# Two chunks instead of one at each visit of a linear-attention and MLP kernel to its attention part

## The chip, the cores and the metric

The kernel runs on one core of a Trainium2 chip. The metric is the device time of one execution in microseconds (us). Before the change its median over three runs is 209.67 us (209.66 to 209.96).

The engines are named as in the profile: PE (matmuls; PEld is its weight load), ACT (activations and copies), DVE and POOL (elementwise work; POOL also issues the loads from memory), and SP (issues transposing DMAs and the stores).

## The reference

```python
# attention, per batch b and head h, blocks of 64 positions, state kept from block to block
intra = (qb @ kb.T * Dmask) @ vb           # Dmask: lam ** (i - j) for i >= j, else 0
inter = (qb * lam_pow) @ kv_state
out[:, :, sl] = intra + inter
kv_state = lam_block * kv_state + (kb * rev_pow).T @ vb
...
x = out.transpose(0, 2, 1, 3).reshape(B * S, H * D)      # 3072 tokens x 512
g = gelu(x @ w_in)                                       # exact gelu, 512 -> 2048
return g @ w_out                                         # 2048 -> 512
```

q, k and v are 4 batches x 8 heads x 768 positions x 64; the output is 3072 x 512 in float32. The kernel works in bf16 with float32 sums.

## The kernel before, in words

**Chunks and groups.** The kernel cuts a sequence into chunks of 128 positions. A chunk is one of 4 batches at one of 6 places in the sequence, with all 8 heads, so there are 24 chunks, numbered 4 * place + batch. Four chunks make a group: 512 tokens. The MLP of group g runs on PE while the attention of group g + 1 is slipped in between its blocks of matmuls. Chunks 0 and 1 come before group 0's first block, chunks 2 and 3 between its first blocks.

**MLP blocks.** `mlp_blocks` gives a list of blocks. For groups 1 to 5 these are 16 blocks of the first matrix product (`mm1`: four matmuls of 512 columns into a PSUM bank of the tag `mh`, which has two banks, then a GELU on ACT that empties it, lines 412 and 416) and 14 blocks of `blocks_by_seven` (the second product, done by seven products of half size; 8 matmuls of 256 columns each, line 306; their sums run on DVE). That is 30 blocks, and each counts 2048 in a running cost called `done`. Group 0 has 21 blocks of the first product, then 16 of the second (`mm2`, four matmuls of 512 columns, line 426).

**The attention of one chunk** (n) has these steps:

- `begin` and `dma_transposes` (185-189): SP issues two transposing DMAs, `kT` and then `qT`, from the loaded k and q. Both have three buffers. Chunks 0 to 7 are transposed on PE instead (`transposed`, line 169).
- `decay_v` (163): POOL makes `v_dec` (7 buffers).
- `scores` (191-200): 8 matmuls on half of the array's rows (line 196) into two banks of the tag `sc`; then `masked` twice, a DVE product each (204), which gives `sc_m`.
- `outputs` (222-235): 4 matmuls with the state over the whole array (226) and 8 matmuls on half of the array's columns with `v_dec` and `sc_m` (231), into a bank of the tag `o`; then `empty_outputs` writes the chunk's part of x, by ACT for chunks 0 to 7 (239) and by DVE for the others (241).
- `next_state` (206-220): 4 matmuls (211) into the bank of the tag `t`, and two DVE operations.
- `prefetch` (453): POOL issues the loads of k, q and v of the chunk four numbers on (67).

**What sets the order.** The program is written out by hand: each engine executes its instructions in the order in which Python emits them. For group 0 the dictionary `group0` (546) says before which block a step stands. For the rest, `todo` (568-575) is a sorted list of (place, step, chunk), and a step is emitted before the first block whose `done` has reached its place; `place(g + f)` is the point at the fraction f of group g's blocks. The scores of group g + 1's four chunks stand at four places spread over group g (fractions 0.06 to 0.795 for g > 1, 0.21 to 0.81 for g = 1). Outputs of a chunk stand where the scores of the next one stand, and the last outputs at 0.93. `begin` stands 0.32 of a group ahead of the chunk's scores. The outputs of chunk 7 open group 1, whose first block is split by columns so that its first part does not need chunk 7.

Of the kernel before, what the change touches and what calls it, by code (L numbers as in the profile page):

```python
# [8 lines left out]
F32 = mybir.dt.float32  # L9
BF16 = mybir.dt.bfloat16  # L10
# [5 lines left out]
def kernel(  # L16
# [10 lines left out]
    nc = tc.nc  # L27
# [137 lines left out]
    def transposed(c, name, tag, empty):  # L165

        src, t_ps = getattr(c, name), bank([128, HP, C], BF16, tag, "t_ps")
        for hp in range(HP):
            nc.tensor.transpose(t_ps[:, hp, :], src[:, 2 * hp:2 * hp + 2, :], ident)  # L169
# [14 lines left out]

    def dma_transposes(c):
        c.kT = work_pool.tile([128, HP, C], BF16, tag="kT", name="kT")
        c.qT = work_pool.tile([128, HP, C], BF16, tag="qT", name="qT")
        nc.sync.dma_start_transpose(out=c.kT, in_=c.k.rearrange("p h d -> p (h d)"))
        nc.sync.dma_start_transpose(out=c.qT, in_=c.q.rearrange("p h d -> p (h d)"))

    def scores(c):
        sc_ps = [bank([128, HP, C], F32, "sc", f"sc_ps{hi}") for hi in range(2)]
        for hp in range(HP):
            for hi in range(2):
                p = slice(hi * D, (hi + 1) * D)
                nc.tensor.matmul(sc_ps[hi][:, hp, :], c.kT[p, hp, :], c.qT[p, hp, :], start=True, stop=True)  # L196
        c.sc_m = work_pool.tile([128, HP, 2, C], BF16, tag="sc_m", name="sc_m")
        c.sc_ps = sc_ps
        for hi in range(0 if c.n == 0 else 2):
            masked(c, hi)  # L200

    def masked(c, hi):
# [16 lines left out]
            nc.vector.tensor_mul(new, tmp, lam_blk)  # L219
        states[c.n + M] = new  # L220

    def outputs(c, x_t, off, evacuate=True):
        o_ps = bank([128, HP, C], F32, "o", "o_ps")
        if c.sb > 0:
            for hp in range(HP):
                nc.tensor.matmul(o_ps[:, hp, :], states[c.n][:, hp, :], c.qT[:, hp, :],  # L226
                                 start=(hp == 0), stop=False, skip_group_check=True)
        v = c.v if c.early else c.v_dec
        for hi in range(2):
            for hp in range(HP):  # L230
                nc.tensor.matmul(o_ps[hi * D:(hi + 1) * D, hp, :], v[:, 2 * hp + hi, :], c.sc_m[:, hp, hi, :],  # L231
                                 start=(c.sb == 0 and hp == 0), stop=True, skip_group_check=True)
        c.x_o, c.o_ps = x_t[:, :, off * C:(off + 1) * C], o_ps
        if evacuate:
            empty_outputs(c)

    def empty_outputs(c):
        if c.n < 2 * M:
# [28 lines left out]
    def blocks_by_seven(g, g_t, first):  # L267
# [22 lines left out]
                    g_sum((5, 2, 1, 6, 7)[i - 10], 0)  # L290
            return both

        paired = [kf for k in range(KH) for kf in (k, k + KH)]
        blocks = [(with_sums(i, first[kf][0]), first[kf][1]) for i, kf in enumerate(paired)]
# [103 lines left out]
    def mlp_blocks(g):  # L398
        T = M * C
        x_t = xT[g]  # L400
        g_t = g_pool.tile([128, NK2, T], BF16, tag="g", name="g_t")

        def mm1(kf, ks=1, cols=slice(0, T)):
            n = cols.stop - cols.start

            def run():
                h_ps = bank([128, ks, n], F32, "mh", "h_ps")
                parts = [(0, T - C), (T - C, T)] if g == 1 and kf == 0 else [(0, n)]
                for k in range(ks):
                    for lo, hi in parts:  # L410
                        for ki in range(NK1):
                            nc.tensor.matmul(h_ps[:, k, lo:hi], w_in_t[:, ki, (kf + k) * 128:(kf + k + 1) * 128],  # L412
                                             x_t[:, ki, cols.start + lo:cols.start + hi],
                                             start=(k == 0 and lo == 0 and ki == 0), stop=(ki == NK1 - 1),
                                             skip_group_check=True)
# [73 lines left out]
    causal(1)  # L489
    keep_warm(2)  # L490
    scores(c)
    for hi in range(2):
        masked(c, hi)
# [5 lines left out]
    outputs(live[0], xT[0], 0)  # L499
# [5 lines left out]
    outputs(live[1], xT[0], 1)  # L505
    c = early(2)
    transposed(c, "k", "mh", copy)
    transposed(c, "q", "mo", copy)
# [31 lines left out]
    x1 = lambda n: outputs(live[n], xT[1], n - M)  # L540
# [4 lines left out]
    e = N1  # L545
    group0 = {
        1: [lambda: scores(live[2])],
        5: [lambda: outputs(live[2], xT[0], 2)],
        6: [lambda: next_state(live[0])],
        7: [lambda: next_state(live[1])],  # L550
        8: [lambda: both_transposed(live[3])],
        9: [lambda: next_state(live[2])],
        10: [lambda: scores(live[3])],
        12: [lambda: outputs(live[3], xT[0], 3)],
        17: [lambda: next_state(live[3])],
        e: [w_out_sums, lambda: decay_v(live[4], nc.vector)],
        e + 8: [lambda: transposes(live[4])],
        e + 9: [lambda: scores(live[4])],
        e + 10: [lambda: x1(4), lambda: transposes(live[5])],
        e + 11: [lambda: scores(live[5])],  # L560
        e + 12: [lambda: x1(5), lambda: transposes(live[6])],
        e + 13: [lambda: scores(live[6])],
        e + 14: [lambda: x1(6), lambda: transposes(live[7])],
        e + 15: [lambda: scores(live[7])],
    }

    BEGIN, STATE, SCORES, OUTPUTS = 0, 1, 2, 3
    todo = [(total, -OUTPUTS, 2 * M - 1)]
    for n in range(2 * M, NCH):
        g, i = n // M - 1, n % M  # L570
        first, apart = (0.21, 0.2) if g == 1 else (0.06, 0.245)
        at = first + apart * i
        todo += [(place(g + at - (0.28 if n == 2 * M else 0.32)), -BEGIN, n), (place(g + at), -SCORES, n),
                 (place(g + (at + apart if i < M - 1 else 0.93)), -OUTPUTS, n)]
    todo += [(place(n // M + (0.01, 0.12, 0.18, 0.24)[n % M]), -STATE, n) for n in range(M, NCH - M)]
    todo.sort()

    def step(minus_kind, n):
        kind = -minus_kind
        if kind == BEGIN:  # L580
            live[n] = begin(n)
            dma_transposes(live[n])
            decay_v(live[n], nc.gpsimd)
        elif kind == SCORES:
            scores(live[n])
            prefetch(n + M)
        elif kind == STATE:
            next_state(live[n])
        else:
            outputs(live[n], xT[n // M], n % M)  # L590

    done = 0
    for g in range(NG):
        if g + 1 < NG:
            alloc_x(g + 1)
        for i, (run, cost) in enumerate(mlp_blocks(g)):
# [1 line left out]
                for act in group0.get(i, []):  # L598
                    act()
            while todo and todo[0][0] <= done:  # L600
                step(*todo.pop(0)[1:])
            run()
            done += cost
        for item in [t for t in todo if t[2] // M == g + 1 and t[1] != -STATE]:
            todo.remove(item)
            step(*item[1:])


# [28 lines left out]
```

## Time and profile before

| | |
|---|---|
| median of three runs | 209.67 us (209.66 to 209.96) |
| the profiled execution's own time | 209.99 us |
| its span, first to last instruction | 208.2 us |
| PE busy | 200.3 us, 96% of the span |
| DVE / POOL / ACT busy | 139.0 / 97.1 / 81.7 us |
| group 1's first MLP block starts | 53.5 us |
| groups 2, 3, 4, 5 start | 84.9, 116.0, 147.1, 178.1 us |
| bytes moved by DMA | 24.65 MB in 102370 packets |

The span is 1.8 us shorter than the execution's own time; what lies around it belongs to launch and end. Busy matmuls overlap in the records (a matmul is 379 ns long but the next one starts 216 ns after it), so lengths on PE are taken from start to start, or from the chain of waits, which cuts the overlaps. A few matmul records are missing in the trace, so a piece shown as x7 may have held 8.

### The profile page before, as it was taken

The page shows a single profiled execution, that of the slowest core. Times are in us where ns is not written, and L with a number is a line of the kernel's source. Part 1 is how long each engine was busy: PE and PEld are TensorE (multiplying, and loading weights), DVE is VectorE, ACT ScalarE, POOL GpSimd, SP SyncE. Part 2 cuts the span into 40 slices and gives each one's busy share as a digit, 9 for nine tenths or more (in the row PEclk, how much of TensorE's full clock was granted, in tenths as well). Part 3 has the DMA queues.
Part 4 walks back from the last instruction along what each step waited for, and adds up shares of the span by engine and source line. Part 5 has one row for each costly group of instructions (what it writes and reads, how often), then busy time and mean ns, then how long its engine had stood idle before and what let it go on. Part 6 is the DMA issues. An engine that isn't in the chain of part 4 may idle for free.

```text
span 208.2 us, 4142 instructions
## 1 busy us (share of the span) xinstructions
PE 200.3 (96%) x1708; PEld 130.5 (63%) x1725; DVE 139.0 (67%) x220; ACT 81.7 (39%) x145; POOL 97.1 (47%) x112
## 2 busy tenths in 40 slices
PE   7889999999999999999999999999999999999992
PEld 2457574465555788654688554688555688544881
DVE  4744525855476789889779689579678579123482
ACT  4966563324555410265420265410365410466200
POOL 8999953799998995499300493000200000000000
PEclk9999999999999999999999999999999999999999
DMA  5999999999999999999930699100651000500014
GB/s 116 155 174 177 200 207 188 154 215 148 151 177 154 153 150 154 233 141 175 155 25 3 219 134 175 29 0 3 227 103 29 0 0 3 201 0 0 3 50 151
DMA packets 102370, 24.65 MB, mean 118 GB/s; under 512 B 92880, under 2 KB 99536, under 8 KB 102352
## 3 DMA queue, kind: packets, MB, share of 16 engines
q0 software_dynamic: 80688, 13.37, 90.2%
q1 hardware_dynamic: 21664, 11.02, 23.5%
q8 instruction: 13, 0.21, 0.4%
q14 instruction: 5, 0.04, 0.1%
HBM read 27.27 MB, written 6.29 MB: 161 GB/s over the span
## 4 chain that ended last, share of the span: by engine, by line
PE 86%; POOL 8%; DVE 3%; issue 1%; POOLq 0%; DVEq 0%
PE h_ps L412 39%; PE p_ps L306 9%; PE r_ps L306 8%; PE q_ps L306 8%; PE o_ps L426 7%; PE o_ps L231 4%; PE s_ps L306 3%; PE sc_ps L196 3%; PE kv_ps L211 3%; POOL w_in_t L88 3%; PE o_ps L226 2%; POOL k_t L67 2%; POOL q_t L67 2%; POOL v_t L67 2%; PE t_ps L169 1%
## 5 line engine op out<-in xcount | busy, mean ns | idle before, releaser
L416 ACT ACTIVATE g_t<-h_ps 128x512 bf16<-128x512 f32 (+2 forms) x101 | 58.2, 576 | 81.2 <-PE h_ps L412 81.0
L412 PE MATMUL h_ps<-x_t,w_in_t 128*128 128x512 bf16 (+3 forms) x446 | 88.7, 343 | 0.6
L412 PEld LDWEIGHTS <-w_in_t 128*128 128x128 bf16 x460 | 40.2, 98 | 36.0 <-issue 0.6
L163 POOL TENSOR_TENSOR v_dec<-v_t,lam_m 128x512 bf16<-128x512 bf16 x23 | 25.2, 1101 | 44.5 <-PE kv_ps L211 42.9
L306 PEld LDWEIGHTS <-g_sum 128*128 128x128 bf16 x400 | 38.6, 98 | 5.2
L281 DVE TENSOR_TENSOR g_sum<-g_t 128x1024 bf16<-128x1024 bf16 x50 | 33.6, 716 | 11.3 <-ACT g_t L416 11.3
L204 DVE TENSOR_TENSOR sc_m<-sc_ps,cmask 128x512 bf16<-128x512 f32 x40 | 25.6, 680 | 2.0 <-PE sc_ps L196 2.0
L67 POOL DMA_DIRECT2D v_t<-in_v_dram x24 | 21.4, 893 | 3.3 <-DMA w_out_t<-in_moe_w_out_dram 2.9
L67 POOL DMA_DIRECT2D k_t<-in_k_dram x24 | 22.2, 924 | 1.7 <-DMA w_out_t<-in_moe_w_out_dram 1.4
L67 POOL DMA_DIRECT2D q_t<-in_q_dram x24 | 21.6, 898 | 2.1 <-DMA w_out_t<-in_moe_w_out_dram 2.1
L306 PE MATMUL r_ps<-w_sum,g_sum 128*128 128x256 bf16 x160 | 19.3, 273 | 0.1
L241 DVE TENSOR_TENSOR x_t<-o_ps,lam_q 128x512 bf16<-128x512 f32 x16 | 11.0, 687 | 10.2 <-PE o_ps L231 10.2
L306 PEld LDWEIGHTS <-g_t 128*128 128x128 bf16 x160 | 15.3, 98 | 3.2
L218 DVE TENSOR_TENSOR tmp<-kv_ps,state 128x512 f32<-128x512 f32 x16 | 11.0, 689 | 7.8 <-PE kv_ps L211 7.8
L426 PE MATMUL o_ps<-w_out_t,g_t 128*128 128x512 bf16 x61 | 14.8, 380 | 0.1
L219 DVE TENSOR_TENSOR state<-tmp,lam_blk 128x512 bf16<-128x512 f32 x16 | 14.4, 901 | 0.5
L306 PE MATMUL p_ps<-w_sum,g_t 128*128 128x256 bf16 x80 | 10.1, 273 | 0.0
L196 PE MATMUL sc_ps<-qT,kT 64*128 64x128 bf16 x192 | 9.5, 218 | 0.3 <-DVE qT L172 0.3
L306 PE MATMUL q_ps<-w_sum,g_t 128*128 128x256 bf16 x80 | 9.7, 273 | 0.0
L470 PE MATMUL idle_ps<-idle 128*128 128x256 bf16 (+1 forms) x33 | 8.4, 393 | 1.2 <-DVE idle L101 1.2
L426 PEld LDWEIGHTS <-g_t 128*128 128x128 bf16 x64 | 5.8, 98 | 6.1
L306 PE MATMUL p_ps<-w_out_t,g_sum 128*128 128x256 bf16 x80 | 9.6, 273 | 0.0
(65 smaller groups left out, 168.0 us busy)
## 6 DMA issues: line engine op xcount, KB each, us to landing
out_dram<-o_sb SPq DMA_DIRECT2D x9, 512.0 KB, 2.8
k_t<-in_k_dram POOLq DMA_DIRECT2D x24, 128.0 KB, 5.9
q_t<-in_q_dram POOLq DMA_DIRECT2D x24, 128.0 KB, 6.1
v_t<-in_v_dram POOLq DMA_DIRECT2D x24, 128.0 KB, 6.2
w_out_t<-in_moe_w_out_dram POOLq DMA_DIRECT2D x4, 512.0 KB, 11.1
w_in_t<-in_moe_w_in_dram POOLq DMA_DIRECT2D x7, 256.0 KB, 7.5
out_dram<-o_sb SPq DMA_DIRECT2D x5, 256.0 KB, 5.7
wide_w<-in_moe_w_in_dram SPq DMA_DIRECT2D x1, 512.0 KB, 4.2
```

What stands on the lines that cost most here:

```text
L67: nc.gpsimd.dma_start(raw[n, name], chunk_of(name, n))
L163: eng.tensor_mul(c.v_dec, c.v, lam_m[:, :, None].to_broadcast((128, H, D)))
L196: nc.tensor.matmul(sc_ps[hi][:, hp, :], c.kT[p, hp, :], c.qT[p, hp, :], start=True, stop=True)
L204: nc.vector.tensor_mul(c.sc_m[:, :, hi, :], c.sc_ps[hi], mask)
L218: nc.vector.tensor_add(tmp, kv_ps, states[c.n])
L219: nc.vector.tensor_mul(new, tmp, lam_blk)
L241: nc.vector.tensor_mul(c.x_o, c.o_ps, lam_q)
L281: nc.vector.tensor_tensor(gsum[i][:, ks, :], g_t[:, ka + k:ka + k + n4, ta], g_t[:, kb + k:kb + k + n4, tb], op=op)
L306: nc.tensor.matmul(o, left[i](k, slice(u * C, (u + 1) * C)), right[i](k), start=(begin and k == 0), stop=(k == KH - 1), skip_group_check=True)
L412: nc.tensor.matmul(h_ps[:, k, lo:hi], w_in_t[:, ki, (kf + k) * 128:(kf + k + 1) * 128], x_t[:, ki, cols.start + lo:cols.start + hi], start ...
L416: nc.scalar.activation(g_t[:, kf:kf + ks, cols], h_ps, ACT.Gelu)
L426: nc.tensor.matmul(om[io], g_t[:, kf, io * C:(io + 1) * C], w_out_t[:, kf, :], start=(kf == 0), stop=(kf == NK2 - 1))
```

## The change

`visit(done, asked)` takes the place of single steps: it emits the outputs of the chunks in `done` (all the matmuls with states, then all those with values, then the emptying) and then the scores of the chunks in `asked`, and after these their four masks, last chunk first, and their prefetches. For this the second chunk's scores go to banks of other tags (`mo`, `mh`, or `t` and `o`) and the second chunk's outputs to `t`. `qT` gets a fourth buffer. B is one block of 30.

- Group 0: chunks 4 and 5 get their scores before block e + 10 and their outputs before e + 13; chunks 6 and 7 get their scores before e + 15.
- Group 1: the first six pairs of `mm1` blocks become 12 half blocks of 256 columns: six on the columns of chunks 4 and 5, then the outputs of chunks 6 and 7 (at 3B), then six on the columns of 6 and 7. Scores of 8 and 9 at 8B; outputs of 8, 9 and scores of 10, 11 at 20B; outputs of 10, 11 and scores of 12, 13 at 26B.
- Groups 2, 3 and 4: outputs of the first two chunks and scores of the last two at 9B; outputs of these and scores of the next group's first two at 26B (in group 4 the outputs alone).
- Of the scores made at 26B, the masks stand apart: at 26B, 28B, and at 1B and 2B of the next group.
- `begin` of a group's first two chunks stands at 0.57 and 0.60 (before the block at 18B) of the group before, that of its last two at 0.00 and 0.04 of the group itself; for chunks 8 to 11 at -0.07, 0, 0.13 and 8B.

```diff
-        dst = work_pool.tile([128, HP, C], BF16, tag=name + "T", name=name + "T")
+        dst = work_pool.tile([128, HP, C], BF16, tag=name + "T", name=name + "T", bufs=4 if name == "q" else 3)
...
-    def scores(c):
-        sc_ps = [bank([128, HP, C], F32, "sc", f"sc_ps{hi}") for hi in range(2)]
+    def scores(c, tags="sc sc", mask=True):
+        sc_ps = [bank([128, HP, C], F32, tag, f"sc_ps{hi}") for hi, tag in enumerate(tags.split())]
...
+    def outputs(*chunks):
+
+        for c, tag in zip(chunks, ("o", "t")):
+            from_states(c, tag)
+        for c in chunks:
+            from_values(c)
+        for c in chunks:
             empty_outputs(c)
...
-            return blocks_by_seven(g, g_t, [(mm1(kf), 4 * T) for kf in range(NK2)])
+            paired = [kf for k in range(NK2 // 2) for kf in (k, k + NK2 // 2)]
+            plan = [(kf, 1, slice(0, T)) for kf in paired]
+            if g == 1:
+                plan = [(kf, 1, slice(0, T // 2)) for kf in paired[:6]]
+                plan += [(kf, 1, slice(T // 2, T)) for kf in paired[:6]] + [(kf, 1, slice(0, T)) for kf in paired[6:]]
...
         e + 8: [lambda: transposes(live[4])],
-        e + 9: [lambda: scores(live[4])],
-        e + 10: [lambda: x1(4), lambda: transposes(live[5])],
-        e + 11: [lambda: scores(live[5])],
-        e + 12: [lambda: x1(5), lambda: transposes(live[6])],
-        e + 13: [lambda: scores(live[6])],
-        e + 14: [lambda: x1(6), lambda: transposes(live[7])],
-        e + 15: [lambda: scores(live[7])],
+        e + 9: [lambda: transposes(live[5])],
+        e + 10: [lambda: visit([], [4, 5], "t o")],
+        e + 11: [lambda: transposes(live[6])],
+        e + 13: [lambda: visit([4, 5], [])],
+        e + 14: [lambda: transposes(live[7])],
+        e + 15: [lambda: visit([], [6, 7], "t o")],
...
+    def visit(done, asked, banks="mo mo", mask=True):
+        outputs(*[live[n] for n in done])
+        for n, tags in zip(asked, ("sc sc", banks)):
+            scores(live[n], tags, mask=False)
+        for n in reversed(asked if mask else []):
+            for hi in range(2):
+                masked(live[n], hi)
+        for n in asked:
             prefetch(n + M)
...
+    B = 1 / (NK2 + 14)
+    for g in range(1, NG - 1):
+        n = (g + 1) * M
+        for i, w in enumerate((0.11, 0.14, 0.19, 0.24) if g == 1 else (0.01, 0.12, 0.18, 0.24)):
+            at(g + w, lambda i=i, g=g: next_state(live[g * M + i]))
+        if g == 1:
+            for i, w in enumerate((-0.07, 0.0, 0.13)):
+                begin_at(g + w, n + i)
+            visit_at(g + 8 * B, [], [n, n + 1])
+            begin_at(g + 8 * B, n + 3)
+            visit_at(g + 20 * B, [n, n + 1], [n + 2, n + 3], banks="mh mh")
         else:
+            for i in (2, 3):
+                begin_at(g + (i - 2) * 0.04, n + i)
+            visit_at(g + 9 * B, [n, n + 1], [n + 2, n + 3])
+        later_on = [n + M, n + M + 1] if g < NG - 2 else []
+        for i, c_n in enumerate(later_on):
+            begin_at(g + 0.57 + 0.03 * i, c_n)
+        visit_at(g + 26 * B, [n + 2, n + 3], later_on, masks=(g + 26 * B, g + 28 * B, g + 1 + 1 * B, g + 1 + 2 * B))
+    at(1 + 3 * B, lambda: visit([2 * M - 2, 2 * M - 1], []))
```

More of the change, by code (lines that the diff above doesn't have):

```diff
@@ L198, in scores @@
         c.sc_ps = sc_ps
-        for hi in range(0 if c.n == 0 else 2):
+        for hi in range(2 if mask else 0):
             masked(c, hi)
@@ L220, in next_state, with from_states, from_values @@
         states[c.n + M] = new
-    def outputs(c, x_t, off, evacuate=True):
-        o_ps = bank([128, HP, C], F32, "o", "o_ps")
+    def from_states(c, tag):
+        c.o_ps = bank([128, HP, C], F32, tag, "o_ps")
         if c.sb > 0:
             for hp in range(HP):
-                nc.tensor.matmul(o_ps[:, hp, :], states[c.n][:, hp, :], c.qT[:, hp, :],
+                nc.tensor.matmul(c.o_ps[:, hp, :], states[c.n][:, hp, :], c.qT[:, hp, :],
                                  start=(hp == 0), stop=False, skip_group_check=True)
+    def from_values(c):
         v = c.v if c.early else c.v_dec
@@ L291, in with_sums @@
             return both
-        paired = [kf for k in range(KH) for kf in (k, k + KH)]
-        blocks = [(with_sums(i, first[kf][0]), first[kf][1]) for i, kf in enumerate(paired)]
+        done = [cost for _, cost in first]
+        blocks = [(with_sums((sum(done[:i]) + 4 * M * C - 1) // (4 * M * C), run), cost)
+                  for i, (run, cost) in enumerate(first)]
         left = {1: lambda k, t: gsum[1][:, k, t], 2: lambda k, t: gsum[2][:, k, t],
@@ L407, in run @@
                 h_ps = bank([128, ks, n], F32, "mh", "h_ps")
-                parts = [(0, T - C), (T - C, T)] if g == 1 and kf == 0 else [(0, n)]
                 for k in range(ks):
[L410 to L415, printed above, removed]
+                    for ki in range(NK1):
+                        nc.tensor.matmul(h_ps[:, k, :], w_in_t[:, ki, (kf + k) * 128:(kf + k + 1) * 128],
+                                         x_t[:, ki, cols], start=(k == 0 and ki == 0), stop=(ki == NK1 - 1),
+                                         skip_group_check=True)
                 nc.scalar.activation(g_t[:, kf:kf + ks, cols], h_ps, ACT.Gelu)
@@ L498 @@
     transposed(c, "q", "mo", copy)
-    outputs(live[0], xT[0], 0)
+    outputs(live[0])
     nc.scalar.copy(w_in_t[:, :, :256], wide_w)
@@ L504 @@
     make_lam_blk()
-    outputs(live[1], xT[0], 1)
+    outputs(live[1])
     c = early(2)
@@ L557, with at, begin_at, run @@
         e + 8: [lambda: transposes(live[4])],
-        e + 9: [lambda: scores(live[4])],
-        e + 10: [lambda: x1(4), lambda: transposes(live[5])],
-        e + 11: [lambda: scores(live[5])],
-        e + 12: [lambda: x1(5), lambda: transposes(live[6])],
-        e + 13: [lambda: scores(live[6])],
-        e + 14: [lambda: x1(6), lambda: transposes(live[7])],
-        e + 15: [lambda: scores(live[7])],
-    }
[L567 to L580, printed above, removed]
+        e + 9: [lambda: transposes(live[5])],
[4 more added lines that the diff above has]
+        e + 15: [lambda: visit([], [6, 7], "t o")],
+    }
+    todo = []
+    def at(when, run):
+        todo.append((place(when), run))
+    def begin_at(when, n):
+        def run():
             live[n] = begin(n)
@@ L583, in step, with visit_at @@
             decay_v(live[n], nc.gpsimd)
-        elif kind == SCORES:
-            scores(live[n])
-            prefetch(n + M)
-        elif kind == STATE:
-            next_state(live[n])
-        else:
-            outputs(live[n], xT[n // M], n % M)
+        at(when, run)
+    def visit(done, asked, banks="mo mo", mask=True):
[6 more added lines that the diff above has]
+        for n in asked:
+            prefetch(n + M)
+    def visit_at(when, done, asked, banks="mo mo", masks=None):
+        at(when, lambda: visit(done, asked, banks, masks is None))
+        if masks:
+            for w, (n, hi) in zip(masks, [(n, hi) for n in asked for hi in range(2)]):
+                at(w, lambda n=n, hi=hi: masked(live[n], hi))
+    B = 1 / (NK2 + 14)
[9 more added lines that the diff above has]
+            visit_at(g + 20 * B, [n, n + 1], [n + 2, n + 3], banks="mh mh")
+        else:
+            for i in (2, 3):
[6 more added lines that the diff above has]
+    at(1 + 3 * B, lambda: visit([2 * M - 2, 2 * M - 1], []))
+    todo.sort(key=lambda t: t[0])
     done = 0
@@ L600 @@
             while todo and todo[0][0] <= done:
-                step(*todo.pop(0)[1:])
+                todo.pop(0)[1]()
             run()
             done += cost
-        for item in [t for t in todo if t[2] // M == g + 1 and t[1] != -STATE]:
-            todo.remove(item)
-            step(*item[1:])
+    assert not todo
 _INS = ['q', 'k', 'v', 'lam', 'moe_w_in', 'moe_w_out']
```

17 lines of the change are left out of this document (8 added, 9 removed).

## The prediction, made before the changed kernel was run

> **What bounds the kernel now.** I read the engines' busy shares first, then the chain of waits, then the waits of PE, then SP's queue.
>
> ```profile
> PE 200.3 (96%) x1708; PEld 130.5 (63%) x1725; DVE 139.0 (67%) x220; ACT 81.7 (39%) x145; POOL 97.1 (47%) x112
> ```
>
> PE is never long without work, and in all it waits for others for under 3 us by the records. So the time is the length of PE's stream, and the change counts by what it takes out of the stream and by the waits that it puts in. The granted clock is 0.998, so no durations change with it. The chain of waits (start, length, what) shows what an attention visit costs in group 2:
>
> ```profile
> 86.12 0.86 PE h_ps L412 x4
> 86.98 0.33 PE sc_ps L196 x8
> 87.31 1.83 PE h_ps L412 x8
> 89.14 0.22 PE kv_ps L211 x4
> 89.37 1.73 PE h_ps L412 x8
> ...
> 101.19 0.87 PE p_ps L306 x8
> 102.06 0.22 PE o_ps L226 x4
> 102.28 0.35 PE o_ps L231 x8
> 102.64 0.33 PE sc_ps L196 x8
> 102.97 0.98 PE p_ps L306 x8
> ```
>
> Four matmuls of 128 columns over the whole array take 0.22 (kv_ps). Eight on half of the rows (sc_ps) or columns (o_ps L231) take 0.33 and 0.35: less than 0.44, so two halves run side by side (0.22), and 0.11 to 0.13 is the price of changing the array's shape. Changing back costs 0.10 more (1.83 against 1.73, 0.98 against 0.87). So scores alone cost 0.33 + 0.10 = 0.43, outputs with scores 0.22 + 0.35 + 0.33 + 0.11 = 1.01, outputs alone 0.22 + 0.35 + 0.11 = 0.68.
>
> **What the change takes out.** From chunk 4 on, the kernel before has 8 scores alone, 8 outputs alone, 12 of both: 8 x 0.43 + 8 x 0.68 + 12 x 1.01 = 21.0 us. In group 0's tail the values also wait for their masks:
>
> ```profile
> 49.27 0.22 PE o_ps L226 x4
> 49.50 0.57 PE o_ps L231 x8
> 50.06 0.55 PE t_ps L169 x8
> ```
>
> Here L231 takes 0.57 instead of 0.35. This happens four times (0.55, 0.56, 0.57, 0.57), and once in group 1 (0.54 at 82.58): 1.0 us of stalls. Now there are 3 pairs of scores alone, 3 pairs of outputs alone and 7 visits with both. A second chunk adds 0.22 for each of its steps while the shape stays; with a change of shape of its own it would add up to 0.35 for each half-array step (2.4 us in all). I take 0.22, since the 0.10 to 0.13 show only where the shape changes. So 3 x 0.65 + 3 x 1.12 + 7 x 1.68 = 17.1 us. The gain is 21.0 + 1.0 - 17.1 = **4.9 us**, and the masks of group 0's pairs (four DVE products, one every 0.60, done 2.6 after the scores) now have 3.6 us, so nothing replaces these stalls.
>
> **What group 1's start adds.** Group 0's tail begins at 39.49 as before. It holds 8 blocks (6.91), 4 transposes (1.80), 2 pairs of scores (1.30), 1 pair of outputs (1.12): group 1 starts at 50.6.
> (a) Half blocks. In group 0 sixteen matmuls of 256 columns start at 15.50 and are over at 17.55, 2.05 us, where 16 x 0.109 = 1.75. Two banks: the fourth matmul starts 0.33 into a block, lasts 0.27, GELU takes 0.38, and hand-overs 0.09, so a bank returns after 1.07 while two half blocks take 0.87. The first six lose 0.2 twice, and some 0.05 behind the last copy of group 0; of the second six three next_state matmuls fill all but 0.2. Together 0.65; they run 50.6 to 53.7.
> (b) Outputs of 6 and 7 (to 54.8) stand right before blocks that read their x. ACT copies both, 0.59 each and 0.49 apart (50.10, 50.58), the first from 54.7; x is there at 55.8. PE waits 1.0; queued behind it are all later blocks.
> (c) Second half blocks, 2.62 + 0.67 (next_state) + 0.2, to 59.3; two whole blocks and a next_state, 1.95: the visit for 8 and 9 comes at 61.3, the scores of 9 at 61.6. They need chunk 9's qT:
>
> ```profile
> 53.87 1.37 SPq L188 DMA_TRANSPOSE kT<-k_t  x1
> 55.43 1.88 SPq L189 DMA_TRANSPOSE qT<-q_t  x1
> ```
>
> This is SP's timeline (start, time on SP). The DMA view gives the time from issue to landing, first for that qT, then for one issued at 153.05, when no loads run:
>
> ```profile
> qT<-q_t SPq DMA_TRANSPOSE x1, 9.0
> ...
> qT<-q_t SPq DMA_TRANSPOSE x1, 2.4
> ```
>
> So chunk 9's qT lands at 64.4. Before, nobody noticed: chunk 9's scores stood at 66.83. The issue is not set by PE: SP issues chunk 8's pair at 49.53 and 50.93 when its loads have landed, then group 0's last two stores, then these. POOL's loads up to chunk 11 are issued by 55.7 in either kernel. Moving POOL's v_dec of chunk 10 ahead of chunk 12's loads (58.2 before, some 60.9 after) comes too late to help. PE waits 64.4 - 61.6 = **2.8 us**, and behind it stand group 1's other 22 blocks. Bounds: 0, if qT lands in under 6.2; 3.5, if it takes as long again as the spread of 7.6 to 9.0 seen around it. Since (c) ends at a fixed moment, errors in (a) and (b) are swallowed by it.
>
> [...]
>
> **What the later visits add.** SP's order again: each transpose takes 1.2 to 1.4 there, and behind these wait only the stores at a group's end.
> (d) Chunks 12 and 13 are begun at 18B of group 1, but qT of 12 reuses chunk 8's buffer and kT of 13 that of chunk 10, both free only in the visit at 20B. With the visit's start as 0: SP issues at 0.4, 1.8, 3.1; the scores of 13 come at 1.68 + 6 x 0.873 + 1.34 = 8.3. Chunk 13's qT may take 5.1. Landings were 6.6 to 6.9 at 66 to 73 and 5.0 to 6.0 at 87 to 97, with loads beside them; POOL issues chunks 14 to 17 without a pause here. Bounds 0 and 1.8; I take 5.7, a wait of **0.6**.
> (e) In groups 2 to 4, transposes of the last two chunks are issued at the group's start, behind its store; the scores of the second come 9 x 0.863 + 4 x 0.224 + 1.34 = 10.0 after it. In the trace of before the fourth transpose behind that store was issued at 90.55 and took 5.1 (10.8 after group 2's start at 84.87), at 121.50 and 5.3 (10.8 after 115.96), at 153.05 and 2.4 (8.4 after 147.06). So 0.8 in group 2, 0.8 in group 3, 0 in group 4: **1.6**, with bounds 0 (landings of 2.4) and 4.6 (6.6 in groups 2 and 3, where loads run).
> (f) Banks and DVE. A visit gives DVE up to six operations in a row (6 x 0.60 = 3.6). At 20B g_sum for the product at 24B is queued behind them: done 5.3 after the visit's start, wanted at 5.6 (fifth matmul of that product). Masks at 28B and in the next group's first blocks fall into idle stretches of DVE. The borrowed banks are emptied 2 us or more before their next use, but for `mo` at 26B of group 1, within 0.1. I take 0; from 0 to 1.0, the slip if two more DVE operations come ahead. POOL's loads move by under 3 us, and the chunks that they feed are begun later than that.
>
> **Sum.** -4.9 + 0.65 + 1.0 + 2.8 + 0.6 + 1.6 = +1.75, rounded +1.8. By group starts: group 2 at 64.8 + 8 x 0.863 + 14 x 0.873 + 2 x 1.68 + 0.6 = 87.9 (before 84.9, +3.0), then -0.8 + 0.8, -0.8 + 0.8, and -1.36 in group 4, which together gives +1.7 to +1.8. The profiled execution (209.99, of it 208.2 span) becomes 211.8. The median of the runs was 209.67, so I predict **211.5**.
>
> **Rivals.**
> R1, faster: qT of 9 lands before 61.6, (c) is nothing, (d) and (e) stand: 209.67 + 1.8 - 2.8 = 208.7. For it: quiet landings of 2.4, fewer loads between 58 and 61. Against: k and q around it landed 7.6 to 9.0 after issue, 1.3 to 2.4 apart, so a queue of work stands in front of each. It decides at a landing time of 6.2.
> R2: no transpose is late at all, (c) to (e) vanish: 209.67 - 4.9 + 1.65 = 206.4. Needs landings under 4.1 for the last of each row with loads running; those under 4 so far were the first of a row or came as loads ended.
> R3, slower still: the visits make transposes come in threes and fours, and with loads issued without pause all land after 6.6 or more: (d) 1.8, (e) 2.3 in groups 2 and 3: 209.67 + 1.8 + 1.2 + 3.0 = 215.7; half of this is 213.6. It begins to decide where a group's fourth transpose takes over 4.3 and grows with every us beyond. For it: landings of 8 to 9 when pairs queued behind each other. Against: group starts had no more than 6.6.
> That the visits don't come about is no rival: the order is written by hand.
>
> **Chances.** The forecast (210.3 to 213.0) 0.60, R1 0.17, R2 0.07, R3 0.11, in between R1 and the forecast, within 0.2%, 0.05. The range 208.5 to 213.4 leaves out R2 and most of R3; the likeliest case alone is 210.3 to 213.0. 0.2%, or 0.4 us, is about what a measurement of this kernel can tell from none. Faster 0.24 (R1, R2), same 0.05, slower 0.71 (forecast, R3).
>
> **What would show it.** Group starts at 50.6, 87.9, 119, 150, 180; a wait of scores (L196) for a transpose of nearly 3 us ending near 64.4, and of 0.5 to 1 us at 9B of groups 2 and 3 but not 4; a wait of 1.0 for ACT's x before the seventh half block; visits of 1.68 and 0.65. If the visits are longer, a second chunk changes the shape again. If the wait near 64 is missing, R1 holds; if group 4 waits too, the loads are not the reason.

## The result, and the profile after

The changed kernel takes **219.55 us** (median of 4 executions, 218.79 to 221.04). The kernel before, on the same chip, takes 209.81 (209.66 to 211.36). The ratio is 1.0455, with an interval of 1.038 to 1.053; here and below, ratios and their intervals leave out executions more than 1.5% longer than the fastest of the same kernel. So the change costs 9.7 us where 1.8 were forecast: the direction was right, the size was not, and the time lies outside the range.

The profiled execution took 221.04 us of its own, 11.05 more than that of before (209.99); its span is 219.3 against 208.2. The first lines of its page:

```profile
PE 200.3 (91%) x1728; PEld 133.4 (61%) x1745; DVE 140.2 (64%) x220; ACT 82.7 (38%) x151; POOL 97.3 (44%) x112
...
PE   7599999999869997995999996899999999999993
...
PEclk9999999999997999998799999699999999999999
```

PE is busy for 200.3 us as before, in a longer span. Past the first tenth, its row of slices dips at the 12th, 16th, 19th and 25th slice (5.5 us each), and behind three of these dips the row of the granted clock dips too, lowest at the 13th, 20th and 26th. The dip of PE is a wait, the dip of the clock a slower PE: two losses.

This is the view of PE's waits (us in total, times, longest):

```profile
PE sc_ps L196 <- DMA qT<-q_t: 8.5, 4, 2.5
...
PE h_ps L421 <- ACT x_t L249: 0.9, 1, 0.9
```

Four times the scores wait for a DMA transpose of q; before they never did. PE's timeline (start, length, what) shows the first and the third of them, each between the scores of the two chunks of one visit:

```profile
61.90 0.40 PE L196 MATMUL sc_ps<-qT,kT 64*128 64x128 bf16 x8
64.41 0.40 PE L196 MATMUL sc_ps<-qT,kT 64*128 64x128 bf16 x8 [2.12 <-DMA qT<-q_t]
...
100.45 0.40 PE L196 MATMUL sc_ps<-qT,kT 64*128 64x128 bf16 x8
103.28 0.61 PE L196 MATMUL sc_ps<-qT,kT 64*128 64x128 bf16 x8 [2.44 <-DMA qT<-q_t]
```

Chunk 8 has its scores at 61.90, chunk 9 only at 64.41; chunk 14 at 100.45, chunk 15 at 103.28. The stretches around these two waits show what the clock does (stretch, its length, busy time of PE, PEld, DVE, ACT, POOL with counts, then PE's granted clock, DMA share and GB/s):

```profile
62.00:65.40 3.40, 1.28 (x19) 0.74 (x18) 1.95 (x3) 0.38 (x1) 3.25 (x4) 1.00 2.05 164
65.50:68.90 3.40, 3.40 (x10) 1.22 (x9) 3.40 (x7) 1.19 (x2) 1.04 (x1) 0.50 2.25 157
99.70:103.00 3.30, 1.14 (x28) 0.86 (x26) 1.72 (x3) 0.41 (x1) 3.30 (x4) 1.00 2.12 156
103.10:106.50 3.40, 3.22 (x15) 1.37 (x15) 2.60 (x5) 0.60 (x1) 3.40 (x5) 0.50 1.83 178
```

PE is idle for 2.1 us of 3.4, still at full clock. Then comes a stretch in which it is busy for all of 3.4 us, at a granted clock of 0.50. This happens three times (from 65.5, 103.1 and 137.2), for 3.41 us each.

The difference of 11.05 us, from the starts on PE in both traces:

| part | predicted | measured |
|---|---|---|
| fewer and merged visits, no mask stalls | -4.9 | -5.0 |
| (a) half blocks | 0.65 | 0.7 |
| (b) ACT's x of chunks 6 and 7 | 1.0 | 1.0 |
| (c) chunk 9's qT, group 1 | 2.8 | 2.3 |
| (d) chunk 13's qT, group 1 | 0.6 | 1.7 |
| (e) fourth transpose of groups 2, 3, 4 | 0.8, 0.8, 0 | 2.8, 2.8, 0 |
| (f) banks and DVE | 0 | 0 |
| half clock after (c) and both (e) | no term | 1.7 + 1.3 + 1.1 = 4.1 |
| start-up of this execution; a pause at 50.29 | no term | 0.4; 0.2 |

Waits in the table are counted from the moment at which the scores would have started; the records of idle time show some 0.2 less, because a matmul's record ends later than the next one could start. Of each 2.8 in (e), 2.6 is the wait, and 0.2 is the scores themselves, which already run at half clock. The clock's part is measured on the blocks behind each wait: 8.60 us against 6.91 for as many blocks at full clock, 7.34 against 6.04, 7.18 against 6.04.

### The profile page after: what moved, and what is told of

It is laid out like the page before. It is cut to its first block, busy times and chain, and to the rows that moved or that the text cites. A ratio compares the mean times of both kernels' runs of the same rounds, so it can differ in the third digit from the quotient of the medians.

```text
span 219.3 us, 4189 instructions
## 1 busy us (share of the span) xinstructions
PE 200.3 (91%) x1728; PEld 133.4 (61%) x1745; DVE 140.2 (64%) x220; ACT 82.7 (38%) x151; POOL 97.3 (44%) x112
## 4 chain that ended last, share of the span: by engine, by line
PE 75%; DMA 17%; POOL 3%; SPq 1%; issue 1%; ACT 0%; DVE 0%; POOLq 0%
PE h_ps L421 35%; DMA qT<-q_t 14%; PE r_ps L317 7%; PE q_ps L317 7%; PE p_ps L317 7%; PE o_ps L434 6%; PE s_ps L317 4%; DMA q_t<-in_q_dram 3%; PE sc_ps L196 3%; PE o_ps L233 2%; PE o_ps L226 1%; PE kv_ps L211 1%; POOL k_t L67 1%; PE t_ps L169 1%; SPq L188 1%
## 5 line engine op out<-in xcount | busy, mean ns | idle before, releaser
L424 ACT ACTIVATE g_t<-h_ps 128x512 bf16<-128x512 f32 (+2 forms) x107 | 59.2, 553 | 95.5 <-PE h_ps L421 93.6
L421 PE MATMUL h_ps<-x_t,w_in_t 128*128 128x512 bf16 (+3 forms) x466 | 92.6, 346 | 1.7 <-ACT x_t L249 0.9
L421 PEld LDWEIGHTS <-w_in_t 128*128 128x128 bf16 x480 | 43.7, 100 | 40.0 <-issue 8.1
L291 DVE TENSOR_TENSOR g_sum<-g_t 128x1024 bf16<-128x1024 bf16 x50 | 35.5, 758 | 18.7 <-ACT g_t L424 18.7
L196 PE MATMUL sc_ps<-qT,kT 64*128 64x128 bf16 x192 | 8.9, 224 | 8.8 <-DMA qT<-q_t 8.5
L219 DVE TENSOR_TENSOR state<-tmp,lam_blk 128x512 bf16<-128x512 f32 x16 | 13.7, 856 | 0.5
L196 PEld LDWEIGHTS <-kT 64*128 64x128 bf16 x192 | 6.1, 96 | 11.7 <-issue 9.5
L251 DVE TENSOR_TENSOR x_t<-o_ps,lam_q 128x512 bf16<-128x512 f32 x16 | 10.3, 685 | 2.4 <-PE o_ps L233 2.4
L355 DVE TENSOR_TENSOR o_sb<-f_e,p_ps 128x512 f32<-128x512 f32 x5 | 3.4, 686 | 11.1 <-issue 8.3
L317 PE MATMUL s_ps<-w_sum,g_sum 128*128 128x256 bf16 x80 | 9.6, 273 | 0.0
```

Source lines behind the costliest of these rows:

```text
L291: nc.vector.tensor_tensor(gsum[i][:, ks, :], g_t[:, ka + k:ka + k + n4, ta], g_t[:, kb + k:kb + k + n4, tb], op=op)
L317: nc.tensor.matmul(o, left[i](k, slice(u * C, (u + 1) * C)), right[i](k), start=(begin and k == 0), stop=(k == KH - 1), skip_group_check=True)
L421: nc.tensor.matmul(h_ps[:, k, :], w_in_t[:, ki, (kf + k) * 128:(kf + k + 1) * 128], x_t[:, ki, cols], start=(k == 0 and ki == 0), stop=(ki ...
```

## The experiments

Two questions are open: why the clock falls, and why the transposes are so late. For the clock, theory A says that it falls because PE idles; rival B says that something else that is new in the kernel lowers it (the load that the bunched work puts on the chip). For the transposes, theory C says that the chunk loads of POOL, which run at the same time, delay them (the expectations call this the second half of theory A, and use "rival C" for the idea that DVE holds the visit); rival D says that it is the order of SP's own issues, three or four transposes in a row behind a store. The kernel before took 209.82 to 209.88 in all these comparisons.

**warm** puts 10, 12 and 12 matmuls of zeros in front of the scores of chunks 9, 15 and 19, into a bank that the scores then overwrite. Nothing is left out.

```diff
+        for _ in range(warm):
+            nc.tensor.matmul(sc_ps[0].rearrange("p h c -> p (h c)"), idle[:, :128], idle, start=True, stop=True)
...
-            scores(live[n], tags, mask=False)
+            scores(live[n], tags, mask=False, warm={9: 10, 15: 12, 19: 12}.get(n, 0))
```

> 34 matmuls of 512 zero columns stand right before the scores of chunks 9 (10 of them), 15 and 19 (12 each), so that PE works while it waits for qT; they write into a bank that the scores overwrite. Theory A (the waits for qT leave PE idle for over 2 us of a 3.4 us stretch, and the clock is then halved for the next stretch): the scores of 9, 15 and 19 start when they did (the transposes set it), but the stretches at clock 0.5 go; granted clock back to about 0.998; two to three stretches of 3.4 us at half speed are worth 1.7 us each, so 214.4 to 216.1 us. Rival B (the clock falls because a visit of 40 to 48 small matmuls is light work, or because of the DMA load beside it, not because PE idles): clock stays at 0.976 to 0.984, time 219.5 us.

Measured: 217.43 us (217.26 to 218.13), ratio 1.0366 [1.0336, 1.0395], 1.3 above the expected range. The profiled executions are 217.26 against 221.04. Its PE timeline, and the stretches with and behind the first wait:

```profile
61.64 2.33 PE L194 MATMUL sc_ps<-idle 128*128 128x512 bf16 x10
64.06 0.40 PE L198 MATMUL sc_ps<-qT,kT 64*128 64x128 bf16 x8
```

```profile
61.30:64.10 2.80, 2.72 (x22) 1.26 (x22) 1.38 (x2) 0.49 (x1) 2.80 (x4) 1.00 1.68 168
64.20:68.00 3.80, 3.75 (x24) 1.76 (x22) 3.53 (x6) 1.79 (x3) 1.40 (x2) 1.00 2.78 146
```

Chunk 9's scores start at 64.06, when their transpose has landed as before, but PE is now busy in the wait and the clock stays at 1.00 in the whole execution. More work on PE made the kernel faster. Rival B falls: the clock fell because PE idled. The profiled execution fell by 3.8 us: 4.1 of the clock and 0.6 of an earlier start-up (the first transposes of group 0's tail at 39.34 instead of 39.92), less some 0.9 that group 3's visit waits longer. This 0.9 is part of why the expectation was missed; another is that three of the changed kernel's four executions show a clock of 0.984, not 0.976, and so had less to win back.

**later13** moves one visit of groups 2 to 4 by four blocks.

```diff
-            visit_at(g + 9 * B, [n, n + 1], [n + 2, n + 3])
+            visit_at(g + 13 * B, [n, n + 1], [n + 2, n + 3])
```

> The visit at 9B of groups 2 to 4 is moved to 13B, nothing else. Theory A: qT of chunks 15 and 19 has landed by then (3.5 us later), both waits of 2.8 us and the one or two half-clock stretches behind them go: 219.5 - 5.6 - 2.4 = 211.5 us, with the waits in group 1 (2.3 and 1.7 us) and one half-clock stretch left. Rival B: the waits go, the clock stays at 0.976 to 0.984: 213.9 us. Rival C (DVE is what holds the visit: its masks and sums in a row): moving the visit next to the sums makes it no better, 218 us or more.

Measured: 212.64 (212.48 to 212.89), ratio 1.0132 [1.0108, 1.0156]. The time lies between theory A's 211.5 and rival B's 213.9; the clock, 0.992 in all four executions, is what A expects and not B. What is left of PE's waits for transposes:

```profile
PE sc_ps L196 <- DMA qT<-q_t: 3.8, 2, 2.0
```

Both are in group 1: (c), and (d), which is now 2.0. The waits of groups 2 and 3 are gone, and with them their two stretches at half clock. The profiled execution fell from 221.04 to 212.56, by 8.5 us: 2.8 + 2.8 of waits, 1.3 + 1.1 of clock and 0.6 of start-up, less 0.3 by which (d) grew, make 8.3. So a wait of 2.8 us cost 4.0: groups 2 and 3 now take 30.3 us each instead of 34.4 and 34.3. One half-clock stretch is left, behind (c). Rival C, DVE, falls as well: it allowed no less than 218.

**early_loads** gives k two more buffers and v_dec two more (and tmp one, for the room), so that POOL's loads run ahead and are over before group 3 starts. SP's order stays as it was.

```diff
-... bufs=10 if name == "k" else 8)
+... bufs=12 if name == "k" else 8)
-... name="v_dec", bufs=7)
+... name="v_dec", bufs=9)
-... name="tmp")
+... name="tmp", bufs=1)
```

> k gets 12 buffers instead of 10 and v_dec 9 instead of 7 (tmp 1 instead of 3 to make room), so that POOL issues the loads of chunks 22 and 23 in group 2 instead of at the start of group 3; the visits stay at 9B. Theory A, second half (the fourth transpose of a group is late because it shares the DMA engines with six loads issued back to back): chunk 19's qT lands in time as chunk 23's does, the wait of 2.8 us in group 3 goes and its half-clock stretch with it, group 2's wait stays between 1 and 3 us: 219.5 - 2.8 - 1.1 = 215.6 us. Rival D (SP's order is to blame: store first, then four transposes 1.3 us apart): group 3's wait stays at 2.8 us, 219.5 us.

Measured: 217.67 (217.26 to 219.84), ratio 1.0392 [1.0329, 1.0454]; the profiled execution is the longest, 219.84. In group 3 the fourth transpose, behind the same store and the same three transposes, has no load beside it. The DMA view (kind, count, us from issue to landing) shows it in this kernel, issued at 133.36:

```profile
qT<-q_t SPq DMA_TRANSPOSE x1, 2.4
```

The same transpose in the changed kernel, issued at 130.59:

```profile
qT<-q_t SPq DMA_TRANSPOSE x1, 7.1
```

The wait of group 3 is gone, and the group takes 30.3 us instead of 34.3. In group 2 the opposite happened. The loads of chunks 14 to 21 now ran from 75 to 100 us with only two breaks of 2 us, where the changed kernel has a break of 7.6 us, from 85.4 to 93.0:

```profile
102.58 0.40 PE L196 MATMUL sc_ps<-qT,kT 64*128 64x128 bf16 x8 [2.38 <-DMA qT<-q_t]
105.37 0.61 PE L196 MATMUL sc_ps<-qT,kT 64*128 64x128 bf16 x8 [2.40 <-DMA qT<-q_t]
```

Both chunks of that visit wait now, and the clock is at 0.50 for 6.8 us, twice 3.41, from 103.1 on, early in the second wait. The group takes 37.5 us instead of 34.4. This is why the total missed its expectation. Both sides speak for theory C: with SP's order unchanged the landing goes from 7.1 to 2.4 when the loads go, and waits double where more loads come. Rival D falls.

**more_bufs** takes away the cause of (d): kT and qT get 5 and 6 buffers (tmp one), so chunks 12 and 13 need no longer wait for the visit at 20B.

```diff
-        c.kT = work_pool.tile([128, HP, C], BF16, tag="kT", name="kT")
-        c.qT = work_pool.tile([128, HP, C], BF16, tag="qT", name="qT", bufs=4)
+        c.kT = work_pool.tile([128, HP, C], BF16, tag="kT", name="kT", bufs=5)
+        c.qT = work_pool.tile([128, HP, C], BF16, tag="qT", name="qT", bufs=6)
```

> kT gets 5 buffers instead of 3 and qT 6 instead of 4 (tmp 1 instead of 3 to make room); places stay. Theory A: the transposes of chunks 12 and 13 no longer wait for the visit at 20B of group 1 and land before the visit at 26B, whose wait of 1.7 us goes; the other waits and the half-clock stretches stay: 217.9 us. If that wait is due to the loads alone and not to the buffers, nothing changes: 219.5 us.

Measured: 217.93, 219.86 and 221.19 (a fourth execution, of 515.77, is left out of the interval), ratio 1.0507 [1.045, 1.0563]. The profiled execution is the first of these. In it the scores at the visit at 26B take 0.60 instead of 2.22, so the buffers were (d)'s cause. It also lacks the half-clock stretch behind chunk 9's wait, which is 1.7 of what it wins. But the other two did not fall, and in the profiled one the wait in group 2 grew from 2.6 to 3.2: PE came 3.6 us earlier there, the transpose landed only 3.0 us earlier (100.20 instead of 103.24).

**out67_early** takes (b) away in the same manner: the outputs of chunks 6 and 7 come one block earlier, at 2B.

```diff
-    at(1 + 3 * B, lambda: visit([2 * M - 2, 2 * M - 1], []))
+    at(1 + 2 * B, lambda: visit([2 * M - 2, 2 * M - 1], []))
```

> The changed kernel with one edit: outputs of chunks 6 and 7 at 2B instead of 3B of group 1. Theory A: the wait for x (1.0 us) falls to about 0.3 us, but PE then comes to the visit at 8B 0.7 us sooner and waits there that much longer for chunk 9's qT, which lands when it did: no change, 219.5 us (half-clock stretches come and go by 1.7 us). If the waits add up, it is 218.8 us.

Measured: 219.22 (218.68 to 219.55), ratio 1.0441 [1.0417, 1.0465]. By the records of idle time, PE's wait at the outputs of 6 and 7 fell from 0.94 to 0.25 (now for a GELU of ACT, no longer for x), and the wait for chunk 9's qT rose from 2.12 to 2.57. The larger part of the gain is swallowed, as the prediction had said of errors in (a) and (b).

Then three kernels each put the cures together, and each missed. **later12_13** is later13 with the first visit of group 1 four blocks later too:

```diff
-            visit_at(g + 8 * B, [], [n, n + 1])
+            visit_at(g + 12 * B, [], [n, n + 1])
```

> As later13 (visits of groups 2 to 4 at 13B), and in group 1 the scores of chunks 8 and 9 stand at 12B instead of 8B. Theory A: chunk 9's qT lands at 64.4 and is wanted at about 65, so the wait of 2.15 us goes and the half-clock stretch behind it (1.7 us): 212.6 - 3.9 = 208.8 us. The wait of some 2 us at 26B of group 1 stays, and may itself halve the clock for one stretch in some executions (then 210.5 us). If the waits were not the whole difference (Rival B: heavier visits, or later masks on DVE), it stays over 211 us.

**later_bufs** adds the buffers of more_bufs to it:

> As later12_13, and kT with 5, qT with 6 buffers (tmp 1 instead of 3). Theory A: the wait at 26B of group 1 goes as well: 208.8 - 2.0 = 206.8 us. If the wait there only moves to the next visits, as it did in more_bufs, whose visits at 9B waited 3.4 and 2.9 us, then 208 to 209 us; at 13B there should be room for that.

**all_mended** adds the move of out67_early to that:

> As later_bufs, and the outputs of chunks 6 and 7 stand at 2B of group 1, so that two half blocks on chunks 4 and 5 run while ACT copies x. Theory A: the wait for x falls from 1.0 to about 0.3 us; all the rest of the prediction's sum is left: 209.7 - 4.9 + 0.65 + 0.3 = 205.7 us, 2% under the kernel before. If the gain of 4.9 us was mis-sized, the time shows by how much, since no transpose is waited for and the clock is whole.

Measured: 213.41 (ratio 1.0166 [1.0121, 1.0211]), 212.89 (1.0161 [1.0115, 1.0207]) and 211.78 (1.005 [1.0019, 1.0082]). Every wait of group 1 for a transpose is gone in them, and each has a new one at 13B of group 2, where later13 had none. PE's timeline of later12_13 and of all_mended there:

```profile
99.78 0.40 PE L196 MATMUL sc_ps<-qT,kT 64*128 64x128 bf16 x8 [1.50 <-DMA qT<-q_t]
103.67 0.61 PE L196 MATMUL sc_ps<-qT,kT 64*128 64x128 bf16 x8 [3.49 <-DMA qT<-q_t]
```

```profile
97.79 0.40 PE L196 MATMUL sc_ps<-qT,kT 64*128 64x128 bf16 x8 [0.71 <-DMA qT<-q_t]
101.08 0.61 PE L196 MATMUL sc_ps<-qT,kT 64*128 64x128 bf16 x8 [2.88 <-DMA qT<-q_t]
```

Chunk 15's scores start at 103.28 in the changed kernel, 105.37 in early_loads, 103.67 here and 101.08 there, however early PE is. Before the change they stood at 109.77, and nobody waited. Group 2 itself started anywhere from 83.8 to 90.7 in these four. So it looks as if from about 50 to 105 us the DMA queues, with loads and transposes together, keep a pace of their own. The expectations had added up the cures of single waits, and most of what PE gained ahead of that pace came back as a wait behind it.

**held_loads** tests the other lever: the changed kernel with k's buffers cut from 10 to 8, to keep the loads of chunks 18 and 19 away from the four transposes.

```diff
-... bufs=10 if name == "k" else 8)
+... bufs=8)
```

> The changed kernel with one edit: k gets 8 buffers instead of 10, so that POOL can issue the loads of chunks 16 and later only when next_state has freed the k of the chunk eight numbers before (16 and 17 in group 2 instead of group 1, 20 and 21 in group 3). All visits stay. Theory A, second half (the loads beside the transposes set when qT lands): at 26B of group 1 only the loads of 14 and 15 run, its wait falls from 1.7 to about 0.5 us; at 9B of groups 2 and 3 the waits fall from 2.8 us to about 1 us, too short to halve the clock: 219.5 - 1.2 - 3.6 - 2.4 = 212.3 us, clock 0.992. If the loads do not matter, 219.5 us. If held loads themselves come too late for the begin of their chunks, new waits show at 26B of groups 2 and 3.

Measured: 217.46 to 222.90, median 220.84, against 212.3 expected; three of the four are left out of ratios, so there is no interval. The loads of chunks 16 and 17, held back too, took the place of 18 and 19 (the first issued at 91.05). The waits for a transpose are 1.9 at 8B and 1.5 at 26B of group 1, 3.3 in group 2 and 2.4 in group 3, and small waits for DVE come up beside them. Fewer buffers shift the collision and don't end it.

**mended_held** joins the two, all_mended with k's 8 buffers:

> all_mended with the same edit (k with 8 buffers). What was left there was one wait of 0.9 + 3.0 us at 13B of group 2, where loads of 14 to 19 had run without a pause, and one half-clock stretch of 1.2 to 1.7 us. Theory A: with the loads of 16 to 19 held back until group 2, chunks 14 and 15 land before 13B, no wait for a transpose is left and the clock stays whole: 211.0 - 3.9 - 1.4 = 205.7 us. If a wait stays at 13B of group 2 or comes up at 26B, 207 to 209 us.

Measured: 208.27 (207.75 to 210.34), ratio 0.994 [0.9916, 0.9965]. This is its second branch, 207 to 209. By the records the wait at 13B of group 2 is 1.3 instead of 0.7 + 2.9, and the clock stays whole behind it; a wait of 1.3 for DVE's g_sum comes up in group 3.

**mended_20** drops that cut and asks later instead: all_mended, k with 10 buffers, and in group 2 alone the visit at 20B.

```diff
-            visit_at(g + 9 * B, [n, n + 1], [n + 2, n + 3])
+            visit_at(g + (20 if g == 2 else 13) * B, [n, n + 1], [n + 2, n + 3], banks="mh mh" if g == 2 else "mo mo")
```

> all_mended (k with 10 buffers again), and group 2's first visit at 20B instead of 13B, its second scores in the banks mh as in group 1. Theory A: the transposes of chunk 15 land near 101 us while loads of 14 to 19 run, whatever PE does; at 20B (start of group 2 at 83.2 + 20.0 + 1.3 = 104.5) nothing waits, so no transpose is waited for anywhere and the clock stays whole: 209.7 - 4.9 + 0.65 + 0.4 = 205.9 us. If another wait of 1 to 2 us comes up (sums on DVE behind six operations of the visit, as the 1.3 us wait for g_sum seen in mended_held), 207 us. If the gain of 4.9 us from fewer changes of shape was too large, over 208 us without any wait in the trace.

Measured: **207.82** (206.87 to 209.47), ratio 0.9897 [0.9875, 0.9919]. It beats both kernels, by 1% and by 5%, and is 1.9 above the 205.9 expected without any wait. The profiled execution is the longest of its six (209.47, span 207.7), so it shows where time is left rather than the whole gain. All that PE waits for longer than 0.3 us once group 1 has begun:

```profile
PE sc_ps L196 <- DVE f_x L369: 1.3, 2, 0.8
...
PE kv_ps L211 <- DVE tmp L218: 0.6, 1, 0.6
```

No scores wait for a transpose, and the clock is 1.0. What is left is term (f): the borrowed bank of the second chunk comes free late, because DVE is behind. In group 1 its `g_sum` at 78.77 and in group 2 the one at 111.03 take 1.4 us instead of 0.7, each beside a `v_dec` of POOL; no run tests whether that slows them. The chain of waits shows a visit in group 3 with no wait in it:

```profile
129.77 0.45 PE o_ps L226 x8
130.22 0.59 PE o_ps L233 x16
130.81 0.55 PE sc_ps L196 x16
131.37 2.70 PE h_ps L421 x12
```

0.45 + 0.59 + 0.55 is 1.59, and with 0.10 to 0.11 for the change back of the array's shape (in this chain s_ps takes 1.85 behind a visit and r_ps, of as many matmuls, 1.75; the 12 matmuls of h_ps take 2.70 here and 2.59 elsewhere), 1.69 to 1.70, about the prediction's price of 1.68. Group 3 takes 30.34 us where it took 31.10 before the change (0.76 less, predicted 0.8), group 4 29.78 (1.31 less, predicted 1.36).

## Why the prediction was wrong in size

**The gain was right.** 4.9 us were forecast and 5.0 found; with a second chunk in a visit, its three steps take 0.45, 0.59 and 0.55 in mended_20 where one chunk's took 0.22, 0.35 and 0.33 before: 0.22 to 0.24 more for each, with no second price of a change of shape. (a), (b) and group 4's zero in (e) were right as well.

**(c) was right in mechanism and moment.** Chunk 9's qT landed at 64.4, as forecast, if with some luck: it was issued 0.55 earlier (54.88) and took 0.5 longer (9.5). PE came to it 0.5 later than forecast, at 62.1, of which 0.4 is the late start of this execution, and waited 2.3. R1, with a landing before 61.6, and R2 fall with it. Why the landing took 9.5 us, where that of a transpose with nothing beside it took 2.4, be it what stands ahead on its own queue, the loads beside it or something else, no run here separates.

**Two steps failed, by some 4 us each. The first is (e):** "So 0.8 in group 2, 0.8 in group 3, 0 in group 4". It read the fourth landing from the rows of before, 5.1 and 5.3. In the changed kernel it is 7.0 and 7.1. The DMA view shows it for group 2 before, issued at 90.55:

```profile
qT<-q_t SPq DMA_TRANSPOSE x1, 5.1
```

and after, issued at 96.26:

```profile
qT<-q_t SPq DMA_TRANSPOSE x1, 7.0
```

The issue came when it was forecast, 5.6 and 5.5 us after the group's start (forecast 5.7), so the miss is the landing. POOL's timeline shows what changed beside it; before:

```profile
89.00 0.88 POOL L67 DMA_DIRECT2D v_t<-in_v_dram  x1
89.89 1.06 POOL L163 TENSOR_TENSOR v_dec<-v_t,lam_m 128x512 bf16<-128x512 bf16 x1
90.88 0.93 POOL L67 DMA_DIRECT2D k_t<-in_k_dram  x1
```

and after:

```profile
94.76 0.88 POOL L67 DMA_DIRECT2D v_t<-in_v_dram  x1
95.62 0.90 POOL L67 DMA_DIRECT2D k_t<-in_k_dram  x1
96.50 0.90 POOL L67 DMA_DIRECT2D q_t<-in_q_dram  x1
```

Before, a v_dec of 1 us stood between the loads of two chunks; after, a visit emits the prefetches of two chunks in a row, and six loads go out without a pause, right beside the four transposes. When the fourth transpose was issued, three loads were on the way (issued and not landed) before the change, and four after it, in both groups. So the change moved the loads that the row depended on, and the row was no longer valid. early_loads shows the dependence on loads (7.1 with them, 2.4 without); that the missing break alone makes the 2 us is read from these rows, and no run tests it by itself. The prediction did ask about the loads, in (f): "POOL's loads move by under 3 us, and the chunks that they feed are begun later than that". It asked whether a load would be late, and not what it would land on. The bounds of the sum held 2.3 a group; the wait was 2.6. R3 had named this mechanism, with a chance of 0.11 and landings of 6.6 or more: it is what happened. With the clock's 4.1 its 215.7 would have been 219.8.

**The second step that failed is "The granted clock is 0.998, so no durations change with it."** It carried the clock of the kernel before over to a kernel with longer waits, where the clock fell to 0.50 behind three of PE's waits. The forecast itself put in a wait of 2.8 us, and no row of before had one like it, so the term should have been bounded. It is 4.1 us in the profiled execution; warm, where PE is busy in these waits and the clock 1.00, shows that the idling is its cause. Idle times of 2.1 us at (c) and of 2.4 in groups 2 and 3 were enough, each with 3.41 us at a clock of 0.50 behind it.

**(d)** was taken at 0.6 and was 1.7, within its bounds of 0 and 1.8: the issues and the scores stood where forecast (3.1 and 8.3 us into the visit at 20B), but the landing took 6.8 instead of 5.7. more_bufs showed its cause to be the one named, the buffers of chunks 8 and 10.

**(f)** was 0 in the changed kernel, as forecast, but with nothing to spare: at 26B of group 1 DVE is done with the borrowed bank at 85.1, just when chunk 13's scores would have started (the prediction's "within 0.1"). In mended_20 it is 0.7 and 0.95 at the visits at 26B of groups 1 and 2, and 0.76 at a next_state: 2.4 in all, more than its bound of 1.0. Whether that comes from the waits that are gone, from the other places of its visits or from the slow g_sums is not shown.

With the table's misses of more than 0.1 in one line: +1.8 forecast, -0.5 for (c), +1.1 for (d), +4.0 for (e), +4.1 for the clock and +0.6 for start-up and pause give +11.1, against 11.05 measured in the profiled execution. The median's 9.7 is lower; by their clocks (0.984 against 0.976) the other three executions lost less to the clock.

What stays open: why the last transpose of group 2's visit lands between 99 and 105 us in every version since the change was read from the landings and not taken apart further. No run has that stretch without any load.

## What to carry to other kernels

Merging two steps to save a fixed cost asks for the second step's operands earlier. Price it by when these land, in the kernel that the change makes, not by landings read in the kernel before: first list which transfers the change moves beside them. A wait on PE can be charged twice, once as idle time and once as half speed behind it: here waits of 2.3 and 2.8 us cost 1.1 to 1.7 us more. And curing waits one by one showed little here (out67_early cured 0.69 us, and 0.45 came back as the next wait), where a queue behind them seems to set the pace: move the visit to where its operand has landed.

## What the runs showed of the hardware

In the changed kernel's profiled execution the three stretches at a clock of 0.50 last 3.413 us each by the trace's records of the clock. They start at 65.51, 103.06 and 137.19, so 37.55 and 34.13 us apart, 11 and 10 times 3.413. PE idled 2.12, 2.21 and 1.90 us in the 3.41 us ahead of each. In all_mended the clock is 0.50 from 100.5 to 103.9, some 0.9 us off the places that this spacing gives for the changed kernel (99.65, 103.06); in the 3.4 us ahead of it PE idled 3.0. Idle time did not always bring such a stretch. In the changed kernel PE idled 1.5 of the 3.4 us from 84.5, and in later13 1.6 of the 3.4 us from 84.8, and the clock stayed at 1.00 there and behind. Waits of 2.0 in more_bufs and of 2.5 in out67_early brought none either: the mean clock of both profiled executions is 0.984, two stretches for three waits of about 2 us or more. So a wait of 2.0 to 2.5 may or may not cost 1.1 to 1.7 us more, and executions of one kernel differ by that (a clock of 0.976 in one of the changed kernel, of 0.984 in three). Each of these numbers is of few cases.

A DMA transpose of 128x512 bf16 between buffers of the chip lands 2.4 us after its issue when no load or store runs. Beside loads of 128 KB each (in the trace the 72 loads are 73728 packets of 128 bytes) the rows here show 5.1 to 9.5. Over all 13 profiled executions, the median landing is 2.45 us for a transpose issued with no chunk load on the way (85 cases), 6.0 with three (39), 6.9 with four or five (167) and 8.3 with six (49).
